# Outer rows of a unit side by side in layer 2, four adds given to transfers, and a new operation order in a two-layer convolution block

## The chip, the cores and the metric

One Trainium2 chip, one of its cores. The time is device microseconds (us) of one execution. Before the change three runs gave 466.6, 465.73 and 466.18 us; the median is 466.18 us. The engines are PE (matrix products), DVE (vector operations), ACT (activations, which also copies results out of PSUM), POOL (GpSimd, which here issues transfers and small memsets) and SP (SyncE, which only issues transfers). Each engine and each issue queue works in program order.

## The reference: what is computed

A residual block on x of shape (2, 512, 64, 64) in bfloat16: group norm with 4 groups, silu, a 3x3 convolution from 512 to 512 channels, the addition of an embedding, a second group norm, silu, a second 3x3 convolution, and the addition of x.

```python
h = conv3(_silu(gn(x, g1, be1)), w1)
emb = _silu(t_emb) @ w_emb
h = h + emb.reshape(B, C, 1, 1)
h = conv3(_silu(gn(h, g2, be2)), w2)
return x + h
```

## The kernel before, in words

**Tiling.** There are 8 chunks: layer (2) times batch item (2) times half image (2). Chunks 0 to 3 are layer 1, chunks 4 to 7 layer 2. A chunk has 4 units, one for each 128 output channels (k = 0 to 3); unit number u runs from 0 to 31, so unit 28 is chunk 7, k = 0. Input channels come in 4 tiles (ct).

**Work of a unit.** The 3x3 convolution is done in a transformed form in the row direction: from groups of input rows, DVE and ACT make six row planes (`rows_a`, `rows_b`), s = 0 to 5, PE multiplies them with transformed weights, ACT evacuates the sums from PSUM, and DVE combines them into four output row groups in a buffer `ys` (lines 998 to 1011; two buffers, used in turn by odd and even units). Planes s = 4 and 5 are the outer ones: they use untransformed weights (`plain_mms`, and in chunk 7 `C_mms` and `D_mms`, made from weights by `outer_weights` on DVE, line 757), and their result is two rows `OO[0]` and `OO[1]` of 520 elements, written by ACT (`evac_o`). They are added to the first and the last group of `ys`. This last addition (lines 1029 to 1040) is either one DVE operation of 128x1040 elements or an *adding transfer*: a DMA issued by POOL with accumulation, written `ar<-ar` in the profile. The table `oacc` says for each chunk in how many of its units the transfer is used; for k = 0 and 1 of chunk 4 it is split into two transfers of one row each (lines 1033 to 1036). In the same way `rows_b` ends by adding a part to planes 4 and 5, by DVE or, for ct below `vacc[c]`, by an adding transfer (lines 714 to 719). In layer 1 `ys` is then stored to `h_scr` and squared on ACT for the second norm; in layer 2 it is added into the output in DRAM by POOL (`out_dram<-ar`).

**Weights in layer 2.** SBUF is one large tile, `ar`, in which everything has a place in elements of 2 bytes. Four regions `UREG[j]`, 10256 elements each, hold the weights of output tile j. In layer 2 elements 0 to 8192 of a region hold transformed weights (`fetch_w2`), 8192 to 9728 half of the streamed weights of the outer planes (`stream_w2`), and from 9728 on there is one outer row. The streams and rows have two slots: even units use regions 0 and 1, odd units 2 and 3. So `OO[1]` lies in the even region of a slot, `OO[0]` in the odd one, 10256 elements on. Each unit's stream is two loads (`ar<-in_w_dram`, 384 KB), one into each region of its slot. In layer 1 the same regions hold other weights, from element 0 to 10240.

**Order.** The kernel first records all its operations with `pl.op`, which works out dependences from exact sets of element numbers, and then emits them in an order written out as a string, `ORDER`: two characters for each operation, read as a number in base 64 (line 97). The instructions reach each engine in that order, and the framework sets the semaphore waits.

```python
def emit(self, order):
    al = "0123456789ABCDEFGHIJKLMNOPQRSTUVWXYZabcdefghijklmnopqrstuvwxyz-_"
    seq = [64 * al.index(order[i]) + al.index(order[i + 1]) for i in range(0, len(order), 2)]
```

Line 347 is the helper of all DVE `tensor_tensor` operations, 351 that of DVE scalings, 370 of ACT, 385 of all transfers and 400 of PE; the profile names these lines.

Of the kernel before, what the change touches and what calls it, by code (L numbers as in the profile page):

```python
# [115 lines left out]
def _idx(off, dims):  # L116
# [28 lines left out]
    'oacc': (4, 4, 4, 0, 4, 4, 4, 0),  # L145
# [13 lines left out]
    'vacc': (0, 3, 3, 3, 0, 0, 0, 0),  # L159
# [8 lines left out]
    "0D0E0F0G0H0I0R0S0T0U0W2T1u0v0y1Q2J1N2c3F1r2M0c0X0a0Z0Y0d0e0f00010b020g13030h14150i0j0k0l0L0m170n0N16180405061907"  # L168
    "081X1Y1Z1A1_0o1a1c0K1B0M1C1D0p0O1E1b1F1d0q0r1e0s1f0_1g1G1H2021231I1h090A0B0V0C3K1i0J22240t0u0w250x0z1j1J2610271k"
    "2e12281K292U1l2A1T2B1m1n112C1o2D1x2E2F1U2G1y2P1z1-1W0-1L1M1O1P1R1S1p1q1s1t1v1w2H2I2K2L2N2O3C3D3E3L0Q2Q1V2R2S0P3M"  # L170
    "4g2W2l2X2m2Y2n3G2Z4T3g4L2f3O2i3P3N3Q2h3S3R2g3V2a3H3a3W3U2o2p3h3i2q2r2s2t2u2v2w2x2y2z3j2-3u4M2d2j4N2k2_304U2b3Z32"
    "314O5P3X3k3c3d3b5H3Y3T4h4P5I4Q5J4k4V334X4W4Y344Z35364b374a3e4S4R3f384d4m4e4n4f6Y4j3v3w3x3y3z3-3_4243443l45464748"
    "494q4r4s4t3m41404B5Q4A6L4i4c5K6D5L5M6F6M6E4u4v3n3o4w4x4-4_50515253543p555c5d5e5f5h2V4l6Z5R3r6a5T7u5U5S5V3q5W5X7v"
    "5Z5a4p3s5N4C3t3I4D4G4F4E7w4H5b8y4o3J56395Y6GB7B84I3A4z574y3B6IB96H5g586N596P5B5C6O5A6Q5D6RBB6T6SBABD6U6K6W6J6X8z"
    "5O6V5i5j5k5l5m5n5o5r5s5t5u5w5x5y5z5-5_60616b6c6d6e6g5v5q5p6h6i6j6k6l6m6n6s6t6u6v6x6y6z6-6_70717262767763BC4JBN7h"
    "BF6fBP4KBH648-65A0686766BJA169A2BR5E8lBOBGBED56A5F6w7P78797A6o7B7C7D7x7y7z7-5G6p8081BQ828384858687BI74737EDDB47Q"
    "6q7RB57S6r7T7UB67V757W7XBL7FD7DF7YBK7ZBS7aBT7b7G7c7d7H7e7K7f7J7g7i8988D66BDEBM7ID97LDH7j7l8A7m7k7n8B7o7pD27tDL7M"
    "BUEeDN8C8D8EDG7_8F8H8I8J8K8L8M8N8O8S8T8U8V8W8X8Y8Z8_908GD88Q8P91929495969798999A9B9G9H9I9J9L9M9N9O9P9Q9R9S8a9W9X"
    "8m8b7O9p9q6CD37r8RD4DIDB7sDA8cDJ7N7q8d8n8f8p8o8q8g8r8e9C9D8t8s8hDP8v9KEgDKDMDC93DOEfEh9UAt9FEi9EDRDQ9T8x8w9V9Y9Z"
# [33 lines left out]
    "dodpdqdrdHdsdtdxdydzd-d5dId_e0e1e2dVcfcedWdYdldXdae4e5e6e7e8e9eAdZeBeEeFeGeHd6agekcydKd8d7dLdNdJdMdOemdPeobuelep"
    "erendRdQeqbvdueIeJeKeLeQeReSeTeUeVeWe3eXeuevewexeyeze-e_eCf1f2f3f4eMeYeNdvdweZf0ePdSeDebeOeaecedeeefegehf5f6f7f8"
    "fCfDfEfFfGfHfIfJfLfMfNfOfPfQfRfSf9fKfTeifBfAfUfsfwftfVfWfXfYfZfafbfcfhfifjfkflfmfnfog1g2g3g4g5g6g7g8gAgBgCgDfdfe"
    "fpfqfvg9gEgFgGgHgLgMejf_g0gNgOgPgQgRgSgUgVgWgXgYgZgagbgegfggghgjgkglgmfgfffrgIfufxfzfygJgTgcgKgdgogpgsgqgrf-gign"
    "gugtgwgygxg_h0gzg-"
# [3 lines left out]
def kernel(  # L221
# [592 lines left out]
    def unit(c, k, opening=0):  # L814
# [572 lines left out]
```

## Time and profile before

| what | value |
|---|---|
| median of three runs | 466.18 us |
| the profiled execution: own time | 466.26 us |
| its span, first to last instruction | 464.5 us |
| PE busy | 447.6 us (96%) |
| DVE busy | 440.9 us (95%) |
| ACT busy | 377.0 us (81%) |
| POOL busy | 65.8 us (14%) |
| mean granted PE clock | 0.994 |
| transfers `ar<-ar` on POOL | 35 |

The page of a profile gives the busy time of each engine, its share in 40 equal slices of the span as digits, and the groups of instructions. A group's row has the line, engine and operation, result and operands with their shapes, the count, and behind the bar the busy time, the mean of one in ns, and the idle time of the engine just before them with what ended it. A row of a timeline gives start and length in us, and in brackets the idle time before and its releaser. "SPq" is the issue queue of SyncE.

### The profile page before, as it was taken

To read this page: it belongs to the slowest core of one execution; us is meant where nothing else is said; L and a number is where in the kernel's file an instruction comes from. 1 tells how busy PE (TensorE), PEld (TensorE's weight loads), DVE (VectorE), ACT (ScalarE), POOL (GpSimd) and SP (SyncE) were. 2 spreads that over 40 slices of the span, in tenths; PEclk is the share of its full clock that TensorE was granted. 3 is DMA by queue.
4 is the path that set the end of the run, shared out by engine and by line. 5 is a ranking of instruction groups with operands and counts; after the bars stand their busy time and mean duration, and the time that the engine had idled before them with its cause. 6 is when DMAs were issued, how large, how long until landed. Compare 5 with 4: busy or idle time off the path is not lost. (4 is left out here: it accounts for less than half of the span.)

```text
span 464.5 us, 8112 instructions
## 1 busy us (share of the span) xinstructions
PE 447.6 (96%) x2891; PEld 281.5 (61%) x2891; DVE 440.9 (95%) x842; ACT 377.0 (81%) x571; POOL 65.8 (14%) x91
## 2 busy tenths in 40 slices
PE   8999999999999999999999999999999999959995
PEld 5744344465554666566556766657776677747882
DVE  4899999999999999999999999999999999949995
ACT  5899999987958999998999898757868798726572
POOL 2210010211021111011000002122221231211210
PEclk9999999999999999999999999999999999998999
DMA  8955682697649387686977687779789777495744
GB/s 314 381 215 168 177 220 71 179 270 212 216 103 295 85 254 230 190 254 198 355 263 275 213 290 177 187 188 195 184 215 268 215 173 180 70 222 136 163 76 92
DMA packets 44472, 94.89 MB, mean 204 GB/s; under 512 B 6544, under 2 KB 18192, under 8 KB 44432
## 3 DMA queue, kind: packets, MB, share of 16 engines
q1 hardware_dynamic: 32208, 77.60, 49.4%
q0 software_dynamic: 11936, 16.78, 23.5%
q8 instruction: 22, 0.36, 0.3%
q14 instruction: 18, 0.15, 0.1%
q10 hardware_dynamic: 288, 0.01, 0.0%
HBM read 62.25 MB, written 31.32 MB: 201 GB/s over the span
## 5 line engine op out<-in xcount | busy, mean ns | idle before, releaser
L400 PE MATMUL psum<-ar 128*128 128x256 f16 (+2 forms) x2771 | 429.7, 317 | 9.6 <-ACT ar L370 5.4
L347 DVE TENSOR_TENSOR ar<-ar 128x1040 f16<-128x1040 f16 (+8 forms) x621 | 409.0, 716 | 12.6 <-DMA ar<-in_w_dram 6.5
L400 PEld LDWEIGHTS <-ar 128*128 128x128 f16 (+1 forms) x2763 | 269.0, 98 | 166.8 <-issue 14.9
L370 ACT ACTIVATE ar<-psum 128x512 f16<-128x512 f32 (+4 forms) x250 | 158.9, 679 | 42.6 <-DVE ar L347 21.9
L370 ACT ACTIVATE ar<-ar 128x512 f16<-128x512 f16 (+6 forms) x146 | 158.9, 1116 | 31.3 <-DVE ar L347 26.6
L370 ACT ACTIVATE ar<-ar,fs 128x2112 f16<-128x2112 bf16 (+1 forms) x32 | 68.8, 2150 | 4.3 <-DVE fs L497 1.9
L385 POOL DMA_DIRECT2D ar<-ar x35 | 38.7, 1126 | 196.6 <-DVE ar L347 80.8
L351 DVE TENSOR_SCALAR ar<-ar 128x512 f16<-128x512 f16 (+3 forms) x90 | 31.4, 370 | 0.4 <-issue 0.2
L385 POOL DMA_DIRECT2D out_dram<-ar x15 | 19.0, 1266 | 55.1 <-DMA ar<-ar 30.0
L370 ACT ACTIVATION_READ_ACCUMULATOR ar<-psum 128x1 f32 x104 | 22.3, 214 | 0.0
L389 POOL MEMSET ar<- 128x65 f16 (+4 forms) x29 | 5.3, 216 | 116.0 <-DVE ar L347 76.8
L400 PEld LDWEIGHTS <-ones_bf 128*128 128x128 bf16 x75 | 7.5, 105 | 6.2 <-issue 3.7
L400 PE MATMUL psum<-ar,ones_bf 128*128 128x260 bf16 x56 | 7.3, 275 | 0.7 <-DMA ar<-in_x_dram 0.7
L400 PE MATMUL psum<-ones_bf 128*128 128x512 bf16 x19 | 6.8, 501 | 1.1 <-DVE ones_bf L404 1.1
L370 ACT ACTIVATION_READ_ACCUMULATOR ar<-ar 128x1 f32 x36 | 7.3, 202 | 0.0
L478 POOL TENSOR_TENSOR fs<-fs 128x1 f32<-128x1 f32 x4 | 3.7, 915 | 17.9 <-DVE fs L476 17.9
L400 PEld LDWEIGHTS psum<-fs,ones_neg 128*128 128x128 f32 x36 | 4.7, 191 | 1.6 <-ACT ar L370 1.0
L400 PE MATMUL psum<-fs,ones_neg 128*128 128x1 f32 (+3 forms) x36 | 4.7, 242 | 0.4 <-ACT ar L370 0.4
L400 PE MATMUL psum<-ar,s_sb 128*2 128x512 bf16 x9 | 2.7, 377 | 0.0
L438 ACT ACTIVATE s_sb<-tparm 128x18 bf16<-128x18 bf16 x1 | 0.2, 219 | 3.0 <-DMA tparm<-in_t_emb_dram 3.0
L432 ACT ACT_TABLE_LOAD x1 | 1.3, 1283 | 1.7 <-PEq L1371 1.7
L437 DVE CAST fs<-gparm 128x16 f32<-128x16 bf16 x1 | 0.2, 174 | 2.5 <-DMA gparm<-in_params_dram 2.5
(54 smaller groups left out, 25.5 us busy)
## 6 DMA issues: line engine op xcount, KB each, us to landing
ar<-in_w_dram SPq DMA_DIRECT2D x36, 384.0 KB, 4.4
ar<-in_x_dram SPq DMA_DIRECT2D x16, 552.5 KB, 4.4
h_scr<-ar SPq DMA_DIRECT2D x16, 520.0 KB, 3.8
ar<-h_scr SPq DMA_DIRECT2D x16, 520.0 KB, 4.4
ar<-ar POOLq DMA_DIRECT2D x31, 260.0 KB, 4.5
out_dram<-in_x_dram SPq DMA_DIRECT2D x30, 260.0 KB, 5.3
out_dram<-ar POOLq DMA_DIRECT2D x15, 520.0 KB, 7.2
ar<-in_x_dram SPq DMA_DIRECT2D x13, 520.0 KB, 6.3
```

What stands on the lines that cost most here:

```text
L347: pl.op("DVE", 0.075 + 0.000521 * out.n, lambda: nc.vector.tensor_tensor(out=out.ap, in0=a.ap, in1=b.ap, op=op), regs(a, b), regs(out), name)
L351: pl.op("DVE", cost or 0.075 + 0.00026 * out.n, lambda: nc.vector.tensor_scalar(out=out.ap, in0=a.ap, scalar1=s, scalar2=None, op0=ALU.mul ...
L370: lambda: nc.scalar.activation(out=out.ap, in_=a.ap, func=func, scale=sc, **kw), regs(*rr), regs(*ww), name)
L385: lambda: eng.dma_start(out=out, in_=in_, **kw), regs(*r), regs(*w), name, lat=3.2 if sw else None, after=after, sw=sw, seq=seq)
L389: pl.op("POOL" if eng == "gpsimd" else "DVE", 0.08 + 0.0005 * out.n, lambda: e.memset(out.ap, v), (), regs(out), name)
L400: nc.tensor.matmul(out.ap, lhsT=lhsT.ap, rhs=rhs.ap, start=st, stop=sp, skip_group_check=True)
L432: nc.scalar.activation(out=fs[:, WARM:WARM + 1], in_=fs[:, WARM + 1:WARM + 2], func=ACT.Silu)
L437: nc.vector.tensor_copy(out=fs[:, GB:GB + 4 * CT], in_=gparm[:])
L438: nc.scalar.activation(out=s_sb[:], in_=tparm[:], func=ACT.Silu)
L478: pl.op("POOL", 0.85, lambda: nc.gpsimd.tensor_tensor(out=F(rs, n).ap, in0=N.ap, in1=F(NEGH, n).ap, op=ALU.pow), regs(N), regs(F(rs, n)), ...
```

## The change

The regions' odd tiles (j = 1 and 3) get their layer 2 weights 528 elements further on, and the odd region's outer row moves to its start, element 0. So the two rows of a unit lie at 9728 of the even region and at 10256, the start of the odd one: 528 apart. The split of the adding transfer in chunk 4 is dropped. Two table entries change: `oacc` of chunk 3 from 0 to 2 (units 3,0 and 3,1 use the transfer), and `vacc` of chunks 1 and 2 from 3 to 4 (ct = 3 too uses it). The string `ORDER` is a new one.

```diff
-    'oacc': (4, 4, 4, 0, 4, 4, 4, 0),
+    'oacc': (4, 4, 4, 2, 4, 4, 4, 0),
...
-    'vacc': (0, 3, 3, 3, 0, 0, 0, 0),
+    'vacc': (0, 4, 4, 3, 0, 0, 0, 0),
...
+    def um_off(j):
+        return UREG[j] + 528 * (j % 2)
+
     def um1(j, ct, kx, pos):
-        return A(UREG[j] + ct * 2048 + kx * 512 + pos * 128, [[1, 128]])
+        return A(um_off(j) + ct * 2048 + kx * 512 + pos * 128, [[1, 128]])
 
     def st_off(s, ct):
-        return UREG[2 * s + ct // 2] + 8192 + (ct % 2) * 768
+        return um_off(2 * s + ct // 2) + 8192 + (ct % 2) * 768
...
-        d = A(UREG[j], [[2048, 4], [1, 1536]])
+        d = A(um_off(j), [[2048, 4], [1, 1536]])
...
-            g = lambda kx: A(UREG[j] + c * 2048 + kx * 512, [[2048, 2], [1, 512]])
+            g = lambda kx: A(um_off(j) + c * 2048 + kx * 512, [[2048, 2], [1, 512]])
...
-            d = A(UREG[2 * s + h] + 8192, [[1, 1536]], BF16)
+            d = A(um_off(2 * s + h) + 8192, [[1, 1536]], BF16)
...
-            g = lambda kx: A(UREG[2 * sl + h] + 8192 + kx * 128, [[384, 4], [1, 128]], BF16)
+            g = lambda kx: A(um_off(2 * sl + h) + 8192 + kx * 128, [[384, 4], [1, 128]], BF16)
...
-            OO = [UREG[2 * (u % 2) + 1] + 9728, UREG[2 * (u % 2)] + 9728]
+            OO = [UREG[2 * (u % 2) + 1], UREG[2 * (u % 2)] + 9728]
...
-        elif k < CFG["oacc"][c] and c == 4 and k < 2:
-            for i in range(2):
-                y_, o_ = A(ys + 24 * RW * i, [[1, PL]]), A(OO[1 - i], [[1, PL]])
-                dma(y_.ap, o_.ap, [o_, y_], [y_], P * 2 * PL, nm + "oa", sw=True, acc=True)
         elif k < CFG["oacc"][c] and not last:
             dma(yo.ap, oo.ap, [oo, yo], [yo], P * 4 * PL, nm + "oa", sw=True, acc=True)
...
-                    memz("gpsimd", A(UREG[j] + 9728 + 32, [[RW, 8], [1, 1]]), "oz")
+                    memz("gpsimd", A(UREG[j] + (0 if j % 2 else 9728) + 32, [[RW, 8], [1, 1]]), "oz")
```

The operations that the prediction follows, with their codes in the two strings (old, new): the odd half of unit 28's stream (cD, cB), the even half (cC, cA), the adding transfer of unit 26, u62oa (af, ad), the last unit's load of x, u73x (gv, gt), and the operands of the adds that become transfers in chunks 1 and 2, ct = 3 (6R and Az in both).

More of the change, by code (lines that the diff above doesn't have):

```diff
@@ L213 @@
[L213 to L217, printed above, removed]
+    "0D0E0F0G0H0I0R0S0T0v1r0c0Z0X0a0Y0d0e0f000102030b130g0h141504050616180i0j0k0L0V0l090A0C0B0W0m170n0N191A07081X1Y1Z"
@@ new lines @@
+    "1_200o0J1B0K0y2J0U1Q1u1N3C3F2M3K2c1C1D0O0p1E0r1F0q1b1a1c1G1d2221240s0M1e1H230t0u250w1f1I1g1h1J0_261i271j2e1k3H28"
+    "292T4T1K101T0P1l2A112B2C1n1m121o2D1x2E1y2F1z2G1-2P1U2Q2f0x0z0-1L1M1O1P1R1S1p1q1s1t1v1w2H2I2K2L2N2O3D3G3L2W2X3E2U"
+    "2V4g3g4O2R2S0Q3I3M1V1W3O3J3N3P2h3Q2Y2Z2l2m2n3h2o2p2q2r2s2t2u2v2w4L2d2b4U4M4N2a3i2i3R3S2g3X3V3U3a3W2j2k3j3k2x2y2z"
+    "2-3u3v3w3x3y3l2_303z3-3_4243444546474849315H3m3T323Z3d3c333b344V374X4W4Y354Z364b4a3Y4h5P384e4k4Q4P4R4f4m3r3n3e3f"
+    "4n5K6L3o5J4A5I4c6D4B5Q41404i4j6F6E393AB75M6M5L4q4r4s4t4u4v4w4x4-4_3p5051525354555R6Y5T5S5U4d5V3q5W5X4l5a6Z4o3s4C"
@@ new lines @@
+    "5b4D4G4F4E4S3t4H5YB94IB8564y57BA3B4z4p6N5Z6P6O6QBB6R6a6T6S5N587u6V597v5C5A5B7w5O6G6H6I5DBD8y6K6U8lBN7h5c5d5e5f5g"
+    "5h5i5j5k5l5m5n5o5r5s5t5u5w5x5y5z5-5_60616b6c6d6eBF6J6WBC6X5pBP5v625q638zBH4KBR8-64A065A1BJ6766A2BG4JBOBEBQBIBS68"
+    "B4DDD55E696g6h6i6j6k6l6m6n6s6t6u6v6x6y6z6w6o6-6_70717276777P78797A7B7C6p6f7D7x7y7z7-8081DF73D7745G7E7FBTDE5F6qDH"
+    "7Q7R7SB57T7U7V6r7WB67X7YBL7ZBK7a757bD97c7d7e7G7f7gDG7i7H7K7J7I7L7j7l7m7k7n7o7pBMBUDJ8283848586878C8D8E8F8H8I8J8K"
+    "8L8M8N8O89D6D8888m8P8AD2DL6A7_6B7MEe9p7q8S8T8U8V8W8X8Y8Z8_9091928G9495969798999A9B9G9H9I9J9LDID37r8B7t8Q6C8aDNEg"
@@ new lines @@
+    "9q8bD48RDB7sDA8n8p8o8q8c8r8g8t8s8d8x7NDK8u93EfDCDMAt8f8eEiDP8v8w8hDO7O9M9N9O9P9Q9C9D9R9S9W9X9Y9K9Z9a9b9c9dA3A4A5"
+    "A6A8A9AAABACADAEAFAKALAM9TANAPAQARAS9UAuDQ9F9fEh9eEuEwEm9E9r9t9s9u9v9w9x9V9-9gDRCr8i9y9h9k9i9j9zAHAG9lCsA79_AvAx"
+    "AwAyAzA_A-AIB2DSAJEbB39mEn8jB0ATAUAVAWAaAbAcAdAeAfAgAhAXBVBWBXBYBaBbBcBdAYBeBfBgBhAOEpEo8kAiAjEO9oAZCQEqGBB1AkCt"
+    "CRAlEjAnAoEkBiBjBlBmBnBoBtBuBvBwByBqBZBpEPAmElEvCTApCUExGDBzB-BxBkB_C0C1C2C3C6C7C8C9CCCDC5CECFDTDUDVDWDYDZDaDbDc"
+    "DdDeDfCvCVCwCuCxCzCyEyEcD1EdEsErEzC_E-BsD0BrC4AqAsCAGJEtE_GKC-GCGLCGGMCSGFGRCWCXCBGNCHG8GPG9GOGACYCICZCaCLDXGECJ"
@@ new lines @@
+    "GHCbGGCcEQDgDjDiDhDkDlDmDrDsDtDuDwDxDyDzD-D_E0E1E4DnDoE5E6E7EAEBECEDF0F1F2F3F5F6F7F8GTCKESERETEUGVEVEW9nCMCdEYCe"
+    "FxHiHkFyHhArEXGSHjGUDpDqGIE8E3E2GQHpHUDvHrEEGWCfHlCgE9ChGXCiEFHtEZCjEGHmCkEaHqHxCNI3GYFEFDEJFzJ6F_F-G0HnG1EHG3G2"
+    "F9FAFBFCFGFHFIFJFOFPFQFRFTFUFVFWFXFYFZFaFdFeFfFgFKEIEKHVHsF4I5FFFLFSFbFjFkFlFcFmGZGaGbGcGeGfGgGhFhGiGjGkGlGpGqGr"
+    "GsGxGyGzG-HzFnCOJ8HoHyHvClHuG6CmHwI4J7G4CPH-I6FNFMCnCpH_FiI7FoCoI1FpGoFsGuFrCqI0G5ELI2EMGtHWGmGnG7FqI9FtHYHXHZKN"
+    "FuGvHaGwHcHbI8HdHfHgHeGdG_H0H1H2H3H4H5H6H7HAHBHCHDHGHHHIHJIBH8ICIDIEIGIHIIIJIKILIMINIRISITHEIUIZIaIbIcH9IeIfIgIh"
@@ new lines @@
+    "J9HKJAENHFJCHLJDHMHPIPJEIWIQHOJBHNJFJGHQJIIVIOJHLeIANLNMKOKPHRLgLfFvIdIXIYIFIiIjIkIlIoIpIqIrIuIvIwIxJSJTJUJVJXJY"
+    "JZJaJbJcImJdJeJiJjInIsJkJlJqJrJsJtJvJwJxJLKQIyJJKRFwItJKIzI-J1I_J0KTKSKUJgKVJfJnJhJmJ2KXKWJoKbKYJpLhLiJyJzJWJ-J_"
+    "K0K3K4K5K6K9KAKBKCKjKkKlKmKoKpKqKrKsKtKuKvK7JuK1KzK-K_K2MvKDKaJMLkJNKZLjLlLmK8LnKELoKFJOKGJPLpJQHSMwMxOzOyJ3NKMy"
+    "HTOhNFKcOjKIKnKwMzKyKxL0L2L1L5L6L7L8LALBLCLDLELFLGLHLKLLLMLNLQLRLSLTL-L_M0M1M3M4M5L9JRKHLOLsKJM-LJLILUKdL4M_L3N0"
+    "LPLqLVLrNJOiN1OwQ9J4PtPuPvRKQ8RLKKKLKeLZLWN3LYN2LXN4J5N6LaOkM6M7M8M9MAMEMFMGMHMMMNMBMDMJOlMCMOMPMRMSMTMUMVMWMXMY"
@@ new lines @@
+    "MbMcMdMeMhMiMjMkM2MQOnN7OoLbMZMIMLMKMaN5MfNNNONPNQNSNTNUNVNWNXNYNZNbNcOpMlNdNeNgNhNiNjNkNlNmNnNrNsNtNuNvNwNxNyMg"
+    "KfMmOGKgMnMqOHKMMpMoOJOmOKMrKhMsKiOrNGLtOxPwNRLdOLNaR3NINHLcMuSXSWR5MtR4Q7Q6N-N_O0O1O2O3O4NoO5O-O_P0P1P3NfOqLuOu"
+    "OILvOMOsNzO6NqLwNpP4ONPxOtO7LxOOPyOPO8PzOvO9OQLyP-ORP5P6P7P8P9PAPCPDPEPFPHPIPJPKPLPMPNPOPBPSPTPUPVPWPXPYPZPbPcPd"
+    "OCOAPGOBP_PPP2TjN8SFLzODOSQ1R6PaPePfPgPhPiPjQAQBQCQDQFQGQHQIQJQKQLQMQOQPQQQRQTQUQVQWQXQYQZQaQeQfQgQhQiN9OTPRQ0NA"
+    "OUQ2NBOVPQR7NCOWPkR9OXPlNDPmOESHRJSGQNOYR8OZQ5OaRATiUvRIQSPoPnPpQERBTRSUSIOFUuQ4Q3PqRCRDNEPrTTTSQbQjQkQlQnQoQpQq"
@@ new lines @@
+    "QrQsQtQuRMRNRORPQmQvRRRSRTRURVRWRXRYRaRbRcRdRfRgRhRiW5W4PsSVQdQcREQwRHRGSJSKSLQxSMRFRQRZReSNQ_QyQ-QzObSOSPR0SQST"
+    "SSOcOdOfOeUdThRjRkRlRmRqRrRsRtRuRvRwRxRzR-R_S0RnS1S2S3S4SYSZSaSbSdSeSfSgShSiSjSkSmSnSoS5RyR1R2TgUeXHUfXGRoOgTURp"
+    "SRS6S7TVS8SlSBScSpSrSsStSuSvSwSxSyT0T1T2T3T4T5T6T7T9TATBTCTDTETFTGTkTlTmTnSAS9SzTXTWTYSCTZTaS_S-SqT8THUgTpTqTrTs"
+    "TtTuTvTwTyTzT-T_U1U2U3U4U5U6U7U8UCUDTbTITcTJUhTKTLTMTxU9TfTNUiTOUjTeUkUlTdUAVpVqVrUtYWSDW_TPUsYVW3X1SEToUEUFUGUH"
+    "UIUJULUMUNUOU0UKUPUQURUSUwUxUyUzU_V0V1V2V3V4V5V6V8V9VAVBVDUTVEVFVGVHVIVJVKVOVPVQVRVSVTVUVVVsUmUnUBUoUpUUUqVtUrVv"
@@ new lines @@
+    "UVVwVuUWUZTQX0U-X2YBW2V7VxUXUYVCVLVzVyUaV-VNX3VMVXVYVZVaVbVcVWVdVeW6W7W8W9WBWCWDWEWFWGWHWIWKWLWMWNWPWQWRWSWTWUWV"
+    "WWVfWaWbWcWdX4VgX5W1X6UbYDZlXEXFUcYCYEZQazZkVhV_ViW0VlX7VkWAVjWJWXWOX9X8VmXAWZXBXCa-VnYFYHXDZRZSYTVoYUWeWfWgWhWj"
+    "WkWlWmWnWoWpWqXIXJXKXLXNXOXPXQXRXSXTXUXWXXXYXZWiXbXcXdXeWrXfXgXhXiXmXnXoXpXqZTXMXaXrXsXtcIZiahWYYIYGWsXVYJWtYKWu"
+    "YLWxYMYOafWvWwXjXvXwXxXyXzX-X_Y0YXYYYZYaYcYdYeYfYgYhYiYjYlYmYnYoagcJZjdZWyZUY1XuYPXlYNZVXkZWY2ZXY3ZYY4ZaZZZbaiY7"
+    "Y6Y5YkajWzdabuYqYrYsYtYuYvYwYxY_Z0Z1Z2Z3Z4Z5Z6Z8Z9YbYyYpZAZBZCZDZEZFZmZnZoZpZrZsZtZuZvZwZxZyZ-Z_a0a1Y8Z7ZdZGalak"
@@ L218 @@
+    "e7e8e9e1eAeBeCeDeEeFeGeHeIeJeOePeQeReSeTeUeVeseteuevewexeyeWeze_f0f1f2f3f4f5f6fAfBeZedeaeXeLeKe-ebeMeNeYecfCfDfE"
+    "fFfGfHfJfKf7fLfMfNfOfPfQfTfUfVfWfXfYfZfafffgfhfifjfkflfmeeeffIf_g0g1egfRf8f9fSfqfcfnfbfefrfdfufsfoftfpfzdQfvfwg2"
+    "g3g4g5g6g7g8g9gAgBgCgDgEgFgJgKgLgMgNgOgPgQgSgTgUgVgWgXgYgZgGgRfxf-ehgIgagHgbgmgngpgqgogsgrgugcgdgegfghgigjgkfygg"
+    "glgvgxgzgwgyg-"
 )
```

50 lines of the change are left out of this document (5 added, 45 removed).

## The prediction, as it was put on record

> **What bounds the kernel now.** I read the page first: the busy shares, then the forty slices.
>
> ```profile
> PE 447.6 (96%) x2891; PEld 281.5 (61%) x2891; DVE 440.9 (95%) x842; ACT 377.0 (81%) x571; POOL 65.8 (14%) x91
> ...
> PE   8999999999999999999999999999999999959995
> ...
> DVE  4899999999999999999999999999999999949995
> ...
> PEclk9999999999999999999999999999999999998999
> ```
>
> Both PE and DVE are full in nearly every slice, and both dip in one slice, the 36th. From the table of stretches of 12 us I summed the stretches from 96 to 408 us: of 312 us DVE is busy 309.6 and PE 308.7. There is no slack to speak of on either engine, so an operation taken off one of them pays only as far as the other was waiting for it. The dip is another matter. The next view is the table of finer stretches around it, whose columns are busy time and count for PE, weight loads, DVE, ACT and POOL, then the granted clock, the DMA share and GB/s.
>
> ```profile
> 408.50:413.30 4.80, 4.75 (x42) 4.11 (x42) 0.60 (x1) 0.00 (x0) 1.19 (x1) 1.00 0.93 192
> 413.30:417.80 4.50, 0.00 (x0) 0.00 (x0) 2.82 (x5) 1.07 (x2) 0.00 (x0) 1.00 1.03 287
> 417.80:422.50 4.70, 4.62 (x23) 3.11 (x23) 4.70 (x11) 2.53 (x5) 0.00 (x0) 0.64 0.61 198
> ...
> 444.00:454.00 10.00, 10.00 (x94) 8.85 (x92) 8.64 (x15) 6.94 (x10) 2.38 (x2) 1.00 0.39 54
> ```
>
> DVE stops at 409.1, PE runs out of work at 413.3, and after its pause PE has a clock of 0.64: 23 matmuls in 4.62 us (0.20 us each), where the last row has 94 in 10.00 us (0.106 each). The timeline from 400 to 426 us names what DVE waits for, and the same view of SyncE's queue and of POOL says why that came late:
>
> ```profile
> 381.22 1.16 SPq L385 DMA_DIRECT2D out_dram<-in_x_dram  x2
> ...
> 404.89 1.19 POOL L385 DMA_DIRECT2D ar<-ar  x1 [9.26 <-DVE ar L351]
> ...
> 409.06 1.40 SPq L385 DMA_DIRECT2D ar<-in_w_dram  x3
> 409.36 1.19 POOL L385 DMA_DIRECT2D out_dram<-ar  x1 [2.05 <-DMA ar<-ar]
> ...
> 414.98 11.22 DVE L347 TENSOR_TENSOR ar<-ar 128x512 f16<-128x512 bf16 x21 [5.88 <-DMA ar<-in_w_dram]
> ...
> 417.80 4.73 PE L400 MATMUL psum<-ar 128*128 128x256 f16 x23 [4.53 <-ACT ar L370]
> ```
>
> The three loads at 409.06 are the outer-row weights of unit 28 (`stream_w2`, chunk 7, k = 0); `outer_weights` on DVE is the first reader. SP is idle from 382.4 to 409.06. The waits of its queue say on what:
>
> ```profile
> SPq L385 <- DVE ar L347: 170.4, 45, 23.2
> SPq L385 <- DMA ar<-ar: 62.5, 9, 16.1
> ```
>
> The 16.1 us ended with an adding transfer, `ar<-ar`: that of unit 26 (u62oa), issued by POOL at 404.89. POOL's own next instruction (out_dram at 409.36) waits for the same landing. But the program names no such dependence: the stream writes elements 8192 to 9728 of a weight tile, u62oa reads from 9728 up. What fits is that the wait is set by first and last address: in the old layout the two rows read lie 10256 elements apart, and everything between, the odd tile's stream among it, counts as read. Following SP's records from unit 22 on, the odd half of a stream waits there for an earlier adding transfer of its slot and the even half never does; behind the transfers of units 16 and 17, split into one for each row, neither does.
>
> **The change, part by part.** Durations are those of the profiled execution: span 464.5 us, own time 466.26; the 1.76 us around the span stay. That time stands 0.08 us above the median of 466.18.
>
> *Layout.* With 528 elements added in the odd tile, the two rows lie at 9728 of the even tile and at 0 of the odd one, 528 apart, with nothing of another user between. The false waits (62.5 us of SP time) go. All but the last cost nothing now, for DVE and PE were busy through them. The last costs DVE 5.88 us. The order helps as well: read two characters at a time, base 64, the odd stream (cD, now cB) stood at position 2408, right behind u62oa (af, 2407); now it stands at 2342, 136 places ahead of u62oa (2478). It is also moved behind u73x, the last unit's load of x, on SP's queue. That one needs DVE to have read buffer AB[0] for unit tile 7,2; the DVE operations between that release and the first `outer_weights` operation in the new order have 27.4 us in the trace, and a load of this kind lands in 4.4 us (median, page part 6). So the weights are there in time; if that cover were gone, the 5.88 us would be back.
>
> What is late next: from 414.98 DVE runs without a break to 424.67, then one ACT eviction, then PE's last 28.1 us without a break. Moved up by 5.88, that chain still ends after PE: PE has 92 matmuls between 408.53 and 425.83, 9.8 us at 0.106, so it could be done at 418.3, where DVE and ACT allow 419.9. **Stall: −5.9 us**; the slow clock goes with it, but lies under DVE. If DVE comes earlier still, PE sets the limit, at 17.3 − 9.8 = 7.5 us, and with PE's 1.22 us wait on DVE just before (407.3 to 408.5) 8.7.
>
> *Four adds moved off DVE* (chunks 1 and 2, ct 3; units 3,0 and 3,1). The row is
>
> ```profile
> L347 DVE TENSOR_TENSOR ar<-ar 128x1040 f16<-128x1040 f16 x188 | 128.3, 695 | 1.7
> ```
>
> 4 × 0.695 = 2.8 us of DVE. Worth between nothing and 2.6 us: PE's idle time from 96 to 408 is 3.3 us in all, 0.7 of it just before the stall, already counted. I take half the 2.8, **−1.4 us**, because DVE's work ahead of the first `outer_weights` operation is 1.4 us less in the new order (3.2 taken away, 1.8 put ahead). POOL gets four issues of 1.126 us and loses the two of the split in chunk 4; it is busy 14%.
>
> *What the adding transfers make late.* The result was there as DVE ended; now POOL must issue and the transfer must land, 4.5 us at the median. For chunks 1 and 2 PE needs it as the fourth step of the chunk's first unit. In the old run those come at 92.45 and 150.16, with the add ended at 92.03 and 150.10: no lead at all. The new order moves the rows ahead. For chunk 1 the operand (6R) has 6.4 us less DVE work ahead, ready about 82.9, landed about 88: covered by 4 us. For chunk 2 (Az) it is 3.2 us, ready 144.4, behind u12oa's issue on POOL, landed 149.5 to 150: just in time, and PE had 0.5 us of idle there anyway. I take 0, bounds 0 and +2.5 us. Units 3,0 and 3,1 have 23 and 17 us until their buffer is written again: nothing. SP's stores of h behind them stand after the next loads in the new queue.
>
> By the Trainium skill, page "SBUF — State Buffer", section "Who interferes with whom", descriptor generation on GpSimd is locked out while DVE runs an operation of its two-port modes, which speaks against more adding transfers under a full DVE. The trace bounds it: their issues take 0.86 to 1.71 us with DVE full, so by that rule at most 0.85 us more for each of the two that PE waits for, and the sum would be 1.7 us higher.
>
> *The rest of the order.* Loads and fillers are moved in the first 36 us, and the chain of the second norm (gn2_1): ACT now has 2.8 us more ahead of the last square, and PE meets gn2_1 two matmul groups sooner (it waits 0.75 us there now). No row prices this; each could give or cost about 1 us. I take 0.
>
> Sum: 466.26 − 5.9 − 1.4 = **459.0 us**.
>
> **Rivals.** (1) *The adding transfers give part back*: by the 2.5 us, and the DVE relief lost in waits for PE: 466.26 − 5.9 + 2.5 = 462.9. For it: chunk 2 has no lead. Against it: chunk 1 has 4 us. Chance 0.16. (2) *The stream stays late* (the odd half still waits, or SP is held by another load): only the 1.4 us remain, 464.9. Against it: position and layout would both have to fail. Chance 0.05. (3) *Slower*: the two transfers at the chunk starts land late. Landings of POOL's transfers range from 2.8 to 11.8 us. At 11.8 the one of chunk 1 comes about 3 us late and that of chunk 2 about 7, and a PE pause of that length brought the clock to 0.64 for 4.7 us here (1.7 us): 466.26 − 7.3 + 10 + 1.7 = 470.7. It decides from the point where the two waits pass 7.3 us together. The existing transfers of this kind (ct 0 to 2) have 11 us and more between operand and use, so the trace has no case. Chance 0.07. (4) *More*: PE becomes the limit behind the stall (8.7) and all DVE relief counts (2.6): 455.0. Below that, 0.04.
>
> **The numbers.** Forecast (455.0 to 461.5) 0.68, (1) 0.16, (2) 0.05, (3) 0.07, below 455.0 0.04. What this kernel's timing can tell from no change is about 0.2%, 0.9 us. Faster: 0.68 + 0.16 + 0.04, less 0.02 for the upper end of (1), and 0.02 of (2): 0.88; same 0.05 from (1) and (2); slower 0.07. Range: from the lower bound 455.0 to 466.26 − 5.9 + 2.5 + 1 = 463.9.
>
> **What the new profile would show.** Right: no wait of DVE for `ar<-in_w_dram` near the end, the three loads issued some 15 us or more ahead of their reader, SP's waits on `ar<-ar` cut to those of real stores, clock 1.00 throughout the last 60 us, 184 operations in the 1040 row, and PE idle of under 2 us in the last two chunks. Wrong: PE idle at the starts of chunks 1 and 2 ended by `DMA ar<-ar`, or at gn2_1 by ACT; or a DVE wait that has only moved.

## The result, and the profile after

| | before | after |
|---|---|---|
| median, same chip | 466.6 us (7 runs, 465.73 to 468.71) | 463.86 us (7 runs, 463.62 to 464.5) |
| ratio, 95% interval | | 0.9934 [0.9912, 0.9955] |
| profiled execution: own time, span | 466.26, 464.5 us | 464.19, 462.2 us |

The kernel became faster, by 2.7 us between the medians. The forecast was 7.2 us. So more than half of the expected gain did not come, and the question is where it went.

**The stall is gone.** First the table of stretches at the end of the run, in the same windows as before (busy time and count of PE, weight loads, DVE, ACT, POOL; then the granted clock):

```profile
408.50:413.30 4.80, 4.80 (x47) 4.30 (x45) 4.70 (x7) 4.80 (x7) 1.21 (x1) 1.00 0.30 87
413.30:417.80 4.50, 4.50 (x44) 4.04 (x42) 4.50 (x10) 1.82 (x3) 1.19 (x1) 1.00 0.40 59
417.80:422.50 4.70, 4.35 (x40) 3.66 (x39) 4.70 (x10) 2.79 (x5) 0.00 (x0) 1.00 0.81 115
```

Where PE had no matmul at all for 4.5 us before, it is full now, and the clock stays at 1.00. The timeline of SyncE's queue shows the loads of unit 28's outer weights:

```profile
389.13 0.34 SPq L385 DMA_DIRECT2D ar<-in_x_dram  x1
393.67 1.66 SPq L385 DMA_DIRECT2D ar<-in_w_dram  x2
```

They go out at 393.67 and 395.0; the first `outer_weights` operation runs at 413.86, 18.9 us after the second. The table of waits agrees. Of DVE, and then of SyncE's queue:

```profile
DVE ar L347 <- ACT ar L370: 6.3, 5, 2.5
...
DVE ar L347 <- DMA ar<-in_w_dram: 0.3, 1, 0.3
```

```profile
SPq L385 <- DMA ar<-ar: 8.0, 4, 5.5
```

DVE's wait for weights fell from 6.5 us to 0.3 (and these 0.3 lie in the first 36 us, not near the end), SyncE's waits for adding transfers from 62.5 us to 8.0. But the first of these lines has grown: DVE now waits 6.3 us for ACT, where it waited 2.9 before.

**Where the time came back.** The forty slices have it, now with new dips in the middle:

```profile
PE 445.6 (96%) x2891; PEld 280.9 (61%) x2891; DVE 439.0 (95%) x838; ACT 377.5 (82%) x571; POOL 70.3 (15%) x93
...
PE   9989999999999889999999799999999999999995
...
DVE  4799999999999999989997999999999999999995
...
PEclk9999999999999999999999999999999999999999
```

I took DVE's idle time by stretches, from the same table of windows. Of before:

```profile
0.00:36.00 36.00, 33.62 (x214) 19.65 (x215) 27.80 (x82) 27.62 (x32) 6.41 (x20) 1.00 0.77 294
...
100.00:206.00 106.00, 105.44 (x632) 61.74 (x631) 105.16 (x234) 92.41 (x185) 15.27 (x16) 1.00 0.72 202
206.00:300.00 94.00, 93.25 (x620) 60.43 (x619) 93.62 (x157) 84.24 (x135) 7.36 (x17) 1.00 0.77 247
```

Of after:

```profile
0.00:36.00 36.00, 31.64 (x201) 18.63 (x202) 25.78 (x78) 26.37 (x29) 7.24 (x20) 1.00 0.76 293
...
100.00:206.00 106.00, 102.46 (x619) 60.44 (x618) 103.17 (x229) 89.49 (x181) 16.50 (x17) 1.00 0.71 200
206.00:300.00 94.00, 90.89 (x598) 58.35 (x597) 91.27 (x165) 84.17 (x138) 7.40 (x16) 1.00 0.78 240
```

Behind the length of a stretch stand the busy times of PE, PEld, DVE, ACT and POOL, each with its count. The third of them is DVE's: DVE is idle 2.0 us more up to 36 us (10.2 instead of 8.2), 2.0 more from 100 to 206, and 2.35 more from 206 to 300. From 36 to 100 and from 300 to 400 it is idle 0.2 and 0.7 us less (from the same table). That is +5.4 us ahead of the stall. With the stall gone (−5.8 us of DVE idle time behind 400 us) and 1.9 us less DVE work (440.9 to 439.0) the sum is −2.3 us, by which the span became shorter. Busy and idle time of an engine always add up to the span, so this says where the time went and not yet why; what was not forecast is the +5.4.

PE shows the same. The first matmul of unit 7,0 (unit 28), from the start of the span, came at 406.5 us before and comes at 412.4 now, 5.9 us late; that of unit 7,1 at 425.8 before, and at 423.5 now, 2.4 early. So 8.2 us were gained within unit 7,0, and 5.9 lost ahead of it.

The largest single piece is in the timeline of DVE in unit 3,1:

```profile
243.47 0.72 DVE L347 TENSOR_TENSOR ar<-ar 128x1024 f16<-128x1024 f16 x1
246.73 2.44 DVE L347 TENSOR_TENSOR ar<-ar 128x2048 f16<-128x2048 f16 x3 [2.55 <-ACT ar L370]
```

The operation that waits is u31y, the addition that forms two output row groups at once (lines 1009 and 1010 of the changed kernel). What ended its wait is ACT's u32m1, which writes plane 1 of unit 3,2 to `M(1)`, the 512 elements behind `M(0)`. In the old order u31y stands 39 places ahead of u32m1, in the new one 2 behind it. The recorded program names no dependence between the two: u31y reads `M(0)`, `M(2)`, `M(3)` and places in `SD`, not `M(1)`. But its second operand steps between `SD`, which lies ahead of the buffers `M`, and `M(2)`, and between its first and last address lies `M(1)`. This is the shape of the false wait that held SyncE's stream before.

### The profile page after: what moved, and what is told of

The parts are those of the page before. It is cut to its first block, busy times and chain, and to the rows that moved or that the text cites. A ratio compares the mean times of both kernels' runs of the same rounds, so it can differ in the third digit from the quotient of the medians.

```text
span 462.2 us, 8115 instructions
## 1 busy us (share of the span) xinstructions
PE 445.6 (96%) x2891; PEld 280.9 (61%) x2891; DVE 439.0 (95%) x838; ACT 377.5 (82%) x571; POOL 70.3 (15%) x93
## 5 line engine op out<-in xcount | busy, mean ns | idle before, releaser
L385 POOL DMA_DIRECT2D ar<-ar x37 | 41.9, 1134 | 202.0 <-DVE ar L347 105.7
L389 POOL MEMSET ar<- 128x65 f16 (+4 forms) x29 | 6.8, 257 | 103.1 <-DVE ar L347 67.6
```

The source lines that it names most:

```text
L385: lambda: eng.dma_start(out=out, in_=in_, **kw), regs(*r), regs(*w), name, lat=3.2 if sw else None, after=after, sw=sw, seq=seq)
L389: pl.op("POOL" if eng == "gpsimd" else "DVE", 0.08 + 0.0005 * out.n, lambda: e.memset(out.ap, v), (), regs(out), name)
```

## The experiments

Theory: the stall is worth what was forecast; the new order costs DVE and PE waits ahead of it, the greatest of them a second wait set by an operand's span of addresses. Rivals: the adding transfers hold PE (rival 1 of the prediction), the stall was worth less, or the start of the run makes the loss. All runs, with the interval of the ratio to before; each compares with the runs of before on its own chip (medians 466.05 to 466.91 us). Below I give differences of medians; the ratios give differences up to 1.0 us away from them, so only what exceeds that counts:

| run | us | ratio |
|---|---|---|
| e1_layout | 460.73 | 0.9884 [0.9862, 0.9906] |
| e2_early | 460.75 | 0.9885 [0.9860, 0.9909] |
| e3_order | 469.49 | 1.0069 [1.0049, 1.0090] |
| e4_dve_adds | 468.81 | 1.0053 [1.0033, 1.0074] |
| e5_transfers | 474.98 | 1.0181 [1.0163, 1.0199] |
| e6_old_start | 463.33 | 0.9933 [0.9920, 0.9947] |
| e7_m1 | 461.05 | 0.9886 [0.9872, 0.9900] |
| e8_three | 460.51 | 0.9880 [0.9861, 0.9899] |
| e9_k33 | 461.42 | 0.9896 [0.9877, 0.9914] |
| e10_oacc | 462.05 | 0.9912 [0.9895, 0.9929] |
| e11_no_oacc | 465.93 | 0.9999 [0.9987, 1.0012] |
| e12_y_split | 461.20 | 0.9883 [0.9863, 0.9904] |

### Parts of the change: layout, order, transfers

**e1_layout**: the kernel before with the new places alone; old order, old tables, split kept.

```diff
+        return UREG[j] + 528 * (j % 2)
...
-            OO = [UREG[2 * (u % 2) + 1] + 9728, UREG[2 * (u % 2)] + 9728]
+            OO = [UREG[2 * (u % 2) + 1], UREG[2 * (u % 2)] + 9728]
```

> The kernel before with the new layout alone: odd tiles' layer 2 weights 528 on, odd outer row at the tile's start; old order, old tables, the split of chunk 4 kept. Theory (the wait for u62oa comes from the span of addresses, and the order costs what is missing): the loads of unit 28 leave about 20 us sooner, DVE's wait of 5.9 us is gone, and PE gets the 8.3 us that it lagged back in the last chunk: 458 us, ratio 0.982, faster than the changed kernel. Rival A (the stall went because the new order puts the stream 136 places sooner; the layout does nothing): no change, 466.3, ratio 1.00. Rival B (the stall was worth only what the whole change brought, some 2.7 us, because DVE or PE was late by the rest anyway): 463.5, ratio 0.994.

460.73 us, 5.4 us (1.16%) below before and 3.1 below the whole change (2.3 by the ratios). It is faster than the whole change, as expected, but 458 was expected: PE does not get back all that it lagged. Its waits on SyncE:

```profile
SPq L385 <- DMA ar<-ar: 8.9, 3, 5.0
```

62.5 us became 8.9 with no other edit than the places, so the wait was one of addresses. Unit 7,0's loads went out at 390.1, DVE runs through the place of the stall, and unit 7,1 starts 5.0 us earlier than before. DVE is now the engine without gaps, and in unit 7,0 PE waits for it (1.23, 0.39 and 0.36 us). From 408.5 on DVE is full where PE is not:

```profile
408.50:413.30 4.80, 3.80 (x35) 3.40 (x35) 4.80 (x9) 1.75 (x4) 1.19 (x1) 1.00 1.11 155
413.30:417.80 4.50, 3.77 (x32) 2.94 (x31) 4.50 (x11) 2.32 (x4) 0.00 (x0) 1.00 0.58 101
```

**e2_early**: the kernel before, old layout; only the two loads `cD` and `cC` of unit 28's stream stand earlier, some 100 places, ahead of u62oa.

```diff
-a9etesZIaA ... c2ayafcDc4c3YSc7c8cCc6
+a9etescDcCZIaA ... c2ayafc4c3YSc7c8c6
```

> The kernel before with one move in its order: the two stream loads of unit 28 go from behind u62oa to behind pre72 on SP's queue, ahead of u62oa; old layout. Theory: a load that is emitted ahead of the adding transfer cannot wait for it, so the stall goes here too: 458 to 459 us, ratio 0.983; u62oa may then wait for the load, some 5 us, off the path. Rival A (order alone): the same. A rival by which the load waits for something else than u62oa (a queue, buffers of the unit before): 466, ratio 1.00.

460.75 us, the same as the layout, and like it about 2 us above what was expected. SyncE still waits 49.8 us for adding transfers, but no longer there:

```profile
SPq L385 <- DMA ar<-ar: 49.8, 9, 11.1
```

So the late load, and nothing else in the layout, is the gain, and a place ahead of the waiting transfer buys it as well as other addresses do. False waits under cover cost nothing, as forecast.

**e3_order**: the change without the layout (new order, new tables, old places, split kept).

```diff
-        return um_off(2 * s + ct // 2) + 8192 + (ct % 2) * 768
+        return UREG[2 * s + ct // 2] + 8192 + (ct % 2) * 768
...
-            OO = [UREG[2 * (u % 2) + 1], UREG[2 * (u % 2)] + 9728]
+            OO = [UREG[2 * (u % 2) + 1] + 9728, UREG[2 * (u % 2)] + 9728]
```

> The changed kernel with the old layout (weights of odd tiles unshifted, rows 10256 apart, split of chunk 4 as before); new order, new tables. Theory: the new order puts the stream ahead of u62oa anyway, so the end stays without the stall, and the other false waits are under cover: 464 us, equal to the changed kernel within 1 us, ratio to the kernel before 0.995. Rival (layout is needed in this order as well): DVE stall or POOL waits come back, 466 to 470, ratio 1.00 or more.

469.49 us, slower than before: the rival's figure, not the 464 of the theory. The timeline of PE and DVE has the false wait back, one unit earlier: PE now waits for the odd stream of unit 27, and DVE behind it:

```profile
404.83 21.34 PE L400 MATMUL psum<-ar 128*128 128x512 f16 x160 [3.84 <-DMA ar<-in_w_dram]
...
415.25 1.66 DVE L347 TENSOR_TENSOR ar<-ar 128x1024 f16<-128x1024 f16 x3 [3.13 <-ACT ar L370]
```

With e1 this makes a table of two by two, in which the parts add as far as the runs can tell: the layout gives 5.4 us under the old order and 5.6 under the new one (469.49 to 463.86); order and tables cost 3.2 us under the old layout (ratio 1.0069) and 3.1 under the new (460.73 to 463.86; 2.3 by the ratios).

**e4_dve_adds** and **e5_transfers**: the change with the four adds back on DVE, and the layout with the old order and the four adding transfers. The edit of e4 (e5 sets the same two entries the other way, in e1's kernel):

```diff
-    'oacc': (4, 4, 4, 2, 4, 4, 4, 0),
+    'oacc': (4, 4, 4, 0, 4, 4, 4, 0),
...
-    'vacc': (0, 4, 4, 3, 0, 0, 0, 0),
+    'vacc': (0, 3, 3, 3, 0, 0, 0, 0),
```

> The changed kernel with the four adds back on DVE (tables of chunks 1, 2 and 3 as before), new order and layout. If the adding transfers are what ate the gain (PE idle 1.2 us at the start of chunk 2 on ar<-ar): 1 to 2 us faster than the changed kernel, 462.5, ratio 0.990. If the order is what ate it: PE waits elsewhere as before, DVE has 2.8 us more to do, 464 to 466, ratio 0.995 to 1.00.

> The layout alone (460.7) plus the four adding transfers at the places where the adds stood in the old order. Theory (a transfer is only free where the order gives it a lead): in the old order the operand of chunk 1, ct 3 is ready 3.2 us and that of chunk 2 2.6 us before PE wants the sum, a transfer needs about 5.5 us with its issue, so PE pauses about 2.5 us at each of these two chunk starts, of which the 2.8 us of DVE relief gives back some: 462 to 465, slower than the layout alone. Rival (the relief counts in full, as it seemed to in the new order, where taking the transfers away cost 5 us): 457 to 459.

468.81 and 474.98 us, both slower than anything that was expected of them. Both are another two by two with e1 (460.73) and the change (463.86): under the new order the four transfers are worth 4.95 us, under the old order they cost 14.25. Not all of the 4.95 is DVE's work of 2.8 us. In e4's trace PE pauses 2.46 us at 170 and 2.92 us at 262, and in the 3.5 us behind them its clock was 0.56 and 0.52; how much of the loss is this slow clock, no run separates. What e5 lacks is lead. In its timeline POOL issues the transfer for chunk 1 at 91.41, and PE, which needs it at 92.79, pauses until 98.98:

```profile
98.98 7.36 PE L400 MATMUL psum<-ar 128*128 128x512 f16 x30 [6.19 <-DMA ar<-ar]
...
161.75 8.44 PE L400 MATMUL psum<-ar 128*128 128x512 f16 x45 [3.22 <-DVE ar L351]
```

This is the third rival of the prediction, at its price and more (9.4 us in these two pauses, where it had 10, and a clock of 0.50 and 0.54 right behind them), in an order where the lead is missing. In the changed kernel PE runs through the start of chunk 1 without a break, and chunk 2 costs PE one short pause:

```profile
153.34 15.84 PE L400 MATMUL psum<-ar 128*128 128x512 f16 x103 [1.21 <-DMA ar<-ar]
```

**e11_no_oacc**: the change with only the two adds of units 3,0 and 3,1 back on DVE (`oacc` of chunk 3 is 0).

```diff
-    'oacc': (4, 4, 4, 2, 4, 4, 4, 0),
+    'oacc': (4, 4, 4, 0, 4, 4, 4, 0),
```

> The changed kernel with the two adds of units 3,0 and 3,1 back on DVE; the two adding transfers of chunks 1 and 2 (ct 3) stay. DVE has 1.4 us more to do ahead of the second norm. With all four adds back on DVE (e4_dve_adds) the time was 468.8 instead of 463.9, 4.9 us for 2.8 us of DVE work, and the first matmul of unit 4,0 came 5.9 us later. Theory A (DVE is the limit here and the four adds count alike, with what each pushes): about half of the 4.9, so 465.5 to 466.5. Theory B (only the adds at the starts of chunks 1 and 2 count, since PE waits for them there): 463.9 to 464.5. Theory C (the ones ahead of the norm count most, since gn2_1 waits for the last sums): 467 to 468.8.

465.93 us: 2.1 us for 1.4 us of work (3.0 by the ratios), near half of e4's 4.95 (5.5), as theory A had it. It is more than the work itself, and the waits in units 3,1 to 3,3 grow with it. The timeline of DVE and PE of this run:

```profile
247.88 9.11 DVE L347 TENSOR_TENSOR ar<-ar 128x2048 f16<-128x2048 f16 x13 [3.98 <-ACT ar L370]
```

```profile
246.10 13.41 PE L400 MATMUL psum<-ar 128*128 128x512 f16 x84 [1.95 <-ACT ar L370]
262.43 3.86 PE L400 MATMUL psum<-ar 128*128 128x512 f16 x10 [2.92 <-ACT ar L370]
```

The wait of u31y is 3.98 us here instead of 2.55, and PE, too, pauses for ACT in the same place. So DVE, PE and ACT wait for one another in turn around u32m1; that this makes up the rest of the 2.1 us is argued from the traces, not tested.

**e10_oacc**: the layout with the old order, and only these two transfers of the four.

```diff
-    'oacc': (4, 4, 4, 0, 4, 4, 4, 0),
+    'oacc': (4, 4, 4, 2, 4, 4, 4, 0),
```

> The new layout with the old order (e1_layout, 460.73 us), and of the four new adding transfers only the two of units 3,0 and 3,1, whose results are read again 23 and 17 us later. DVE has 2 x 0.695 = 1.4 us less to do, about 100 us ahead of the end of the run. Theory (DVE sets the end in e1_layout, and an adding transfer with such a lead costs nothing): 459.3 us, 1.4 below e1_layout. Rival 1 (PE is as full as DVE there, so relief of DVE alone pays less): 460.3 to 460.8. Rival 2 (a transfer delays what stands behind it, the second norm's sums of units 3,0 and 3,1 on ACT, which now wait for the landing, some 4 to 5 us, before they can square): 461 or more, with PE waiting at gn2_1.

462.05 us, 1.3 us slower than e1 although DVE has 1.4 us less to do. The intervals of the two ratios overlap a little, so that the 1.4 us did not come is surer than that the time grew. Rival 2 was right in its kind. It had put the path through ACT's squares; what the trace shows is SyncE's queue. Timelines of SyncE, of e1 first:

```profile
228.99 0.33 SPq L385 DMA_DIRECT2D h_scr<-ar  x1
229.37 1.48 SPq L385 DMA_DIRECT2D out_dram<-in_x_dram  x2
231.92 3.50 SPq L385 DMA_DIRECT2D ar<-h_scr  x2
236.51 0.33 SPq L385 DMA_DIRECT2D ar<-in_w_dram  x1
236.89 0.64 SPq L385 DMA_DIRECT2D ar<-u_scr  x1
```

and of e10:

```profile
232.98 0.33 SPq L385 DMA_DIRECT2D h_scr<-ar  x1
233.36 1.33 SPq L385 DMA_DIRECT2D out_dram<-in_x_dram  x2
234.81 8.38 SPq L385 DMA_DIRECT2D ar<-h_scr  x2
243.63 0.40 SPq L385 DMA_DIRECT2D ar<-in_w_dram  x1
244.08 0.58 SPq L385 DMA_DIRECT2D ar<-u_scr  x1
```

The store of h has to wait for the transfer's landing and goes out 4.0 us later; SyncE's next load waits for a memset that stands behind the second transfer on POOL; and the load of transformed weights (`ar<-u_scr`) goes out 7.2 us later. In the timeline of DVE:

```profile
253.56 5.54 DVE L347 TENSOR_TENSOR ar<-ar 128x1024 f16<-128x1024 f16 x8 [1.65 <-DMA ar<-u_scr]
```

1.65 us of waiting for 1.4 us of work; the rest of the 1.3 us, about 1 us, is not accounted for. A transfer whose own result has 17 us of lead is not free if it stands ahead of others in a queue.

### The waits inside the new order

**e6_old_start**: the change, with the first 170 operations, up to unit 0,0's first matmuls, in the old order. As a diff of what is emitted:

```diff
-    the first 170 operations: new order
+    the first 170 operations: old order
```

> The changed kernel with the first 170 operations (up to the first matmul of unit 0,0) in the old order, the rest in the new one. Theory (the new start makes PE 2.9 us late at unit 0,0, and nothing gives it back): 461.2, 2.7 us less than the changed kernel, ratio to the kernel before 0.989. Rival (a late start is under the cover of DVE, which limits later): 463.9, no change.

463.33 us, 0.5 below the change by the medians, nothing by the ratios, as the rival had it. The 2.9 us by which PE starts unit 0,0 late in the change are gone here, but right behind the exchanged operations PE waits for ACT:

```profile
40.56 1.50 PE L400 MATMUL psum<-ar 128*128 128x512 f16 x6 [1.91 <-ACT ar L370]
```

At unit 1,0 PE is 0.9 us ahead of the change, and by unit 4,0 it is 8.5 us later than before, as in the change. So taking back the start by itself brings 0.5 us at most. Why no more, by DVE's cover or by the waits that follow, this run does not tell.

**e7_m1**: the change, with ACT's u32m1 (`LO`) behind DVE's u31y (`KJ`).

```diff
-L9JRKHLOLsKJM-LJ
+L9JRKHLsKJLOM-LJ
```

> The changed kernel with one ACT eviction (u32m1) emitted behind u31y on DVE instead of ahead of it. They share no element, but u31y's operands span the buffer that u32m1 writes. Theory (a second wait by span of addresses, 2.55 us of DVE at 244 us, which makes PE late by 2.3 us at 258): DVE's idle at 244 goes, 461.6, 2.3 us less than the changed kernel, ratio 0.9885. Rival (DVE waits there for a true input that ACT has late, or the delay is only handed on): 463.9, no change.

461.05 us, 2.8 below the change (2.2 by the ratios), for one operation moved by two places. In the timelines DVE passes u31y without a break, and PE unit 3,3:

```profile
243.03 8.52 DVE L347 TENSOR_TENSOR ar<-ar 128x1024 f16<-128x1024 f16 x12
```

```profile
249.63 15.61 PE L400 MATMUL psum<-ar 128*128 128x512 f16 x102
```

In the change PE pauses there:

```profile
260.67 3.50 PE L400 MATMUL psum<-ar 128*128 128x512 f16 x15 [2.31 <-ACT ar L370]
```

**e12_y_split**: the order of the change untouched, u32m1 still ahead; u31y alone is written as two additions, whose operands each stay within one buffer.

```diff
-        if CFG["ym"][l] and not last:
+        if CFG["ym"][l] and not last and (c, k) != (3, 1):
```

> The changed kernel in its own order, the scaling u32m1 still ahead of u31y as in the change. Only the DVE addition u31y is written as two additions of 128x1024 (line 1013 and 1014) instead of one of 128x2048 whose operands step from one buffer to the other (line 1009), so that neither operand's span of addresses takes in the buffer that u32m1 writes. In e7_m1 the same wait was avoided by order (461.05 us); this run asks whether it is the span that makes it. Theory (the wait is set by first and last address of an operand): DVE's 2.55 us of idle time at u31y is gone or under 0.5 us, PE's pause of 2.31 us at unit 3,3 is gone, and the time is 461.0 to 461.5, with about 0.1 us for one more instruction. Rival 1 (u31y needs something of ACT's that is late, whatever its operands): the idle time stays and the time is 463.5 to 464.2. Rival 2 (ACT's evictions of unit 3,1 are just behind): the wait moves to the second half and half of the gain is left, 462 to 463.

461.20 us, 2.7 below the change (2.4 by the ratios). The wait is gone though ACT's write still stands ahead:

```profile
242.22 9.19 DVE L347 TENSOR_TENSOR ar<-ar 128x1024 f16<-128x1024 f16 x14
```

So it was the span of the operand that made u31y wait, not anything that it reads. With e1 this shows the same rule in two places of this program: on SyncE's queue for a load, on DVE for an addition.

**e8_three** and **e9_k33**: e6 and e7 together with DVE's copy of the first norm's sums moved up, behind u20s; and then ACT's k33 (`HW`) behind two evictions of unit 2,3.

```diff
+    the first 170 operations: old order
+    u31y ahead of u32m1
+    gn2_0's copy from PSUM (line 468): right behind u20s
```

```diff
-I2EMGtHWGmGnG7
+I2EMGtGmGnHWG7
```

> The changed kernel with the old start, u32m1 behind u31y, and the DVE copy of the second norm's sums of batch 0 (gn2_0, line 468) moved up behind u20s, 5 operations sooner, so that PE's 1.5 us pause at unit 2,1 goes. If the three losses add up: 463.9 - 2.7 - 2.3 - 1.5 = 457.4, ratio 0.981, faster than the layout alone (460.7). If one bound lies behind them all (DVE): 460 to 461.

> The kernel e8_three, with one more move: on ACT, the plane scaling k33 that DVE's row33 needs comes behind the two evictions of unit 2,3 (u23b) instead of ahead of them. Nothing else differs. Theory (what the new order costs is a sum of local waits between PE, ACT and DVE, each of which can be taken away by itself): PE's pause of 2.58 us at unit 2,3's fourth plane, which ended with ACT in e8_three, falls to under 1.8 us, and the time from 460.5 to 459 to 460. Rival (DVE is by now the limit, as in the layout alone at 460.7 us): the pause shrinks but DVE waits longer for k33, and the time stays at 460.2 to 461. A time over 461 would say that ACT's order here was the better one.

460.51 and 461.42 us; both miss their expectation. The waits are not a sum that can be taken away term by term. In e8 PE's pause at 170 us is gone and one at 201 us has grown from 0.79 to 2.58; in e9 that one has shrunk to 0.57 and the next plane waits 2.71, for DVE, which had to wait for k33. Timelines of PE, e8 and then e9:

```profile
203.66 8.55 PE L400 MATMUL psum<-ar 128*128 128x512 f16 x37 [2.58 <-ACT ar L370]
```

```profile
202.11 4.83 PE L400 MATMUL psum<-ar 128*128 128x512 f16 x21 [0.57 <-ACT ar L370]
209.65 2.55 PE L400 MATMUL psum<-ar 128*128 128x512 f16 x18 [2.71 <-DVE ar L347]
```

Five versions lie between 460.5 and 461.2 us (e1, e2, e7, e8, e12), ahead of both kernels, and their intervals overlap. In e1, e2, e7 and e12 DVE has no gap over 0.26 us between 206 and 447 us. That fits DVE setting the end in all of them; no run tests it.

## Why the prediction was right or wrong

- **What bounds the kernel, and the stall: right.** The layout alone gave 5.4 us against 5.9 forecast, and the cause was the one named: e1 removes the false waits, e2 shows that only the last of them mattered, e3 that the order without the layout keeps one. If DVE came earlier still, the prediction gave 7.5 to 8.7 us as the most that PE could gain there: in the changed kernel DVE was earlier relative to PE, and unit 7,0 took 8.2 us less. One reading was off: of the three loads at 409.06 two are unit 28's, and the third is the first of unit 29.
- **The moves of the two loads: right.** 18.9 us from issue to reader; u73x ahead of them did no harm.
- **The transfers at the chunk starts: right in the outcome, partly by luck.** Chunk 1 was covered, chunk 2 "just in time": PE waited 1.21 us, within the bounds of 0 and 2.5. But POOL issued the two at 87.77 and 149.96, where the prediction had them ready at 82.9 and 144.4:

```profile
87.77 0.91 POOL L385 DMA_DIRECT2D ar<-ar  x1 [4.91 <-DVE fs L1234]
149.96 0.91 POOL L385 DMA_DIRECT2D ar<-ar  x1 [3.73 <-DVE ar L347]
```

The prediction counted the work ahead of the operand. The transfer adds into planes 4 and 5, and two further sums of `rows_b` read plane 5 first; the recorded program has the transfer wait for them. The cover held because PE, too, came to the two chunk starts 2.5 us later than before. So the time came near rival 1's 462.9, but not for its reason: there the transfers were to cost what they earned, and they earn 5 us in this order (e4). e5 shows the slow rival as a real mechanism, 14 us where the lead is missing.
- **Relief of DVE: wrong as a term of its own.** I took 1.4 us of 2.8, with bounds 0 and 2.6. Within the new order it is 4.95 (e4, slow clock included), within the old order a loss. A transfer changes the order's slack, and the sum treated the order as fixed. For units 3,0 and 3,1 "nothing" held in the new order, where the stores of h stand behind the next loads: the two transfers earn 2.1 us there (e11). In the old order they have a price, in SyncE's and POOL's queues (e10).
- **The step that failed: "The rest of the order ... each could give or cost about 1 us. I take 0."** It looked at two places, the first 36 us and gn2_1, since they are where operations visibly moved. Measured, DVE was idle 5.4 us more ahead of the stall, and order with tables cost 3.1 to 3.2 us (2.3 by the ratios). The order by itself, without the four transfers, cost 8.1 us (e4 against e1), the slow clock behind its pauses included. Taking back the start, which I had named, brought 0.5 at most (e6). The greatest piece was in a unit that I did not look at: u31y waiting for u32m1, 2.2 to 2.8 us of time (e7, e12). It could have been seen blind: the prediction had found the rule (a wait is set by first and last address) and used it for one stream only. The same question put to each pair of operations that the new order swaps, on ACT and DVE too, finds this pair.
- With measured terms: 466.3 − 5.4 (layout) + 2.8 (u31y) = 463.7, against 463.86. That closes only because the transfers and the rest of the order, which are in neither term, come to nothing together. Without the u31y wait the change stands at 461.05, 2 us above the forecast: e7 has 1.9 us less DVE work than e1 (438.8 and 440.7) and the same time. Where that went (DVE waits in the first 36 us and from 100 to 206, in the change 4.0 us more than before) is named, but e8 and e9 did not get it back; it stays open whether any order can.
- That 463.86 lies at the upper end of the range, 463.9, is luck. This end was built from no relief of DVE, 2.5 us of waiting at the chunk starts and 1 us of order; 1.21 us of the waiting came, and the order cost about 3 with the transfers.
- Of the signs that I had set, the right ones came: no wait for the weights near the end, the loads 18.9 us ahead, 184 operations in the 1040 row, PE idle 0.35 us in the last two chunks, and clock 1.00, but for the last 7.2 us, with nine matmuls, where it was 0.90. Of the 8.0 us that SyncE still waits for adding transfers, 5.5 are one wait between 60 and 80 us. Of the wrong ones two came too: 1.21 us at chunk 2, and "a DVE wait that has only moved".

```profile
L347 DVE TENSOR_TENSOR ar<-ar 128x1040 f16<-128x1040 f16 x184 | 125.6, 698 | 2.7 <-ACT ar L370 1.0
```

## What to carry to other kernels

Where waits are set by an operand's first and last address, an operand that steps over a foreign buffer is a dependence: keep strided pairs side by side, or split the instruction, and look for such pairs wherever an order swaps two operations. A change that comes with a new order is priced as two changes, and "the rest of the order" is a term with bounds of its own: list what the swap makes wait on every engine, not only where operations moved far. Work taken off a full engine is worth its time only if what replaces it has lead in every queue it enters; the same four transfers gave 5 us in one order and cost 14 in another.

## What the runs showed of the hardware

**Short pauses of PE can already cost the clock.** The windows right behind PE's pauses, first of 2.31 us in the changed kernel, then of 2.31 us at the same place in e6, of 2.58 (e8), 2.92 (e11) and 6.19 us (e5); the granted clock is the third number from the end:

```profile
260.67:264.40 3.73, 3.73 (x17) 1.66 (x17) 3.73 (x7) 3.73 (x13) 0.00 (x0) 1.00 0.93 373
```

```profile
259.08:262.70 3.62, 3.62 (x10) 1.37 (x10) 3.62 (x7) 3.62 (x12) 0.00 (x0) 0.55 0.93 373
```

```profile
203.66:207.50 3.84, 3.84 (x11) 1.41 (x11) 3.77 (x9) 3.84 (x10) 1.20 (x1) 0.59 0.49 73
```

```profile
262.43:266.30 3.87, 3.87 (x11) 1.42 (x11) 3.87 (x7) 3.65 (x12) 0.00 (x0) 0.60 0.95 358
```

```profile
98.98:103.70 4.72, 4.72 (x20) 2.88 (x21) 0.00 (x0) 3.22 (x6) 0.00 (x0) 0.50 0.43 131
```

I had reckoned with a slow clock only behind pauses like the 4.5 us of before. Pauses of 2.22 (e4), 2.31 (the change) and 2.71 us (e9) left the clock at 1.00; one of 2.31 (e6), one of 2.46 (e4), one of 2.58 (e8) and two of 2.92 (e4, e11) did not. Between 2.3 and 2.7 us it went either way, and 2.31 us did both, so the length alone does not decide it. The Trainium skill, page "TensorE: Matmul & The Clock Gate", section "What's actually happening", has the array go to half rate after at least one idle window of about 3.4 us. The half rate agrees with the 0.50 of e5; the length does not agree with the 2.31 us of e6, and the measurement decides. What else in the window counts as idle, no run here shows.
